# Loading x and w1 in other pieces, transposing x in pairs and running the first h groups side by side, at the start of a fused SiLU MLP forward and backward

## The chip, the cores and the metric

One core of one Trainium2 chip. The metric is device time of the program in microseconds (us), median of several executions. The profile's span is 1.7 to 2.0 us shorter than that time in all runs but one (2.35 us), because it begins with the first recorded instruction. All times inside the program are counted from the start of the span.

## The reference

Forward and gradients of a two-layer MLP in bfloat16, S = 2048 rows, D = 640, F = 1536:

```python
h   = einsum("bsd,df->bsf", x, w1)
out = einsum("bsf,fd->bsd", silu(h), w2)
# returned: out and the gradients of x, w1, w2 for a given grad_out
```

## The kernel before

TensorE does everything in 128x128 by 128x512 matmuls, 1,440 of them (the last 16 split in two). Rows are worked on in four chunks of 512. Chunk 0 first needs x transposed: four tiles of 128 rows are loaded, transposed on TensorE and copied out of PSUM, the memory that TensorE writes to, into `xT`. Then twelve groups of five matmuls make h. Everything later is long prefetched. These are the parts that matter, with cuts marked.

```python
# NWARM = 26 matmuls on a constant come first, to get TensorE's clock raised
load_x_tile(nc.sync, 0)            # 160 KB each; SyncE's and ScalarE's queue in turn
load_x_tile(nc.scalar, 1)
load_x_tile(nc.sync, 2)
load_x_tile(nc.scalar, 3)
for lo, hi in ((0, 2), (2, DT)):   # w1 rows in tiles of 128 (DT = 5), first 256 columns (FH)
    nc.sync.dma_start(out=w1_nat[:, lo:hi, 0:FH], in_=w1_v[:, lo:hi, 0:FH])
load_w1(FH, FC)                    # columns 256 to 512, all rows
# ... the rest of w1; w2 in two halves; transposed loads

def pe_x_tile(xT, st):             # one tile: 3 + 2 transposes, one copy for each part
    for lo, hi, copy in ((0, DS, nc.vector.tensor_copy), (DS, DT, nc.scalar.copy)):
        tp = ps_h.tile([P, hi - lo, P], dt_in, name="tp", tag="hp")
        for dt_ in range(lo, hi):
            nc.tensor.transpose(tp[:, dt_ - lo, :], x_nat[:, st, dt_ * P:(dt_ + 1) * P], ident[:])
        copy(out=xT[:, lo:hi, st * P:(st + 1) * P], in_=tp[:])

for st in range(STC):
    pe_x_tile(xT_next, st)
for i in range(NFILL):             # 4 fillers that keep TensorE busy
    nc.tensor.matmul(wp[:, 0:P], lhsT=ident[:], rhs=x_nat[:, STC - 1, 0:P], start=True, stop=True)
# ...
for ft in range(FT):               # chunk 0: twelve groups, one after the other
    h_group(ft, xT, aT, ghT)       # 5 matmuls over dt_, then silu, tanh, two VectorE steps
```

## Time and profile before

| | before |
|---|---|
| time, median of 3 runs | 322.19 us (321.62 to 322.34) |
| span of the profiled run | 320.5 us |
| first h matmul | 6.48 us |
| from there to the start of the last VectorE copy | 311.09 us, matmuls without a gap |
| busy share of TensorE | 98% |

The timeline of TensorE before (columns: start, duration, engine, line, operation, out<-in, shapes, count, and in brackets the idle time ahead of it and what ended it; a merged line's duration ends with its last, modelled matmul):

```profile
0.78 2.93 PE L96 MATMUL wp<-const-bfloat16-1.0 128*128 128x128 bf16 x26 [0.78 <-PEq L362]
3.62 0.74 PE L148 MATMUL tp<-ident,x_nat 128*128 128x128 bf16 x10
5.32 0.73 PE L148 MATMUL tp<-ident,x_nat 128*128 128x128 bf16 x10 [0.96 <-DMA x_nat<-in_x_dram]
5.88 0.39 PE L154 MATMUL wp<-x_nat,ident 128*128 128x128 bf16 x4
6.48 13.11 PE L161 MATMUL hp<-xT,w_nat 128*128 128x512 bf16 x58 [0.21 <-ACT xT L149]
19.43 13.11 PE L196 MATMUL hp<-aT,w_nat 128*128 128x512 bf16 x59
```

Phases follow each other at 12.95 us, which is 60 matmuls at 0.216 us. (The trace lacks a few matmul records: 58 and 59 of 60.) So whatever starts h earlier ends the program earlier, one for one. The chain of waits of the first 20 us before, from the x tile's transfer to h (start, duration, what; the lines ahead of and after these are left out, here and below):

```profile
1.19 4.09 DMA x_nat<-in_x_dram
5.27 0.05 issue
5.32 0.47 PE tp L148 x5
5.78 0.02 issue
5.81 0.66 ACT xT L149 x2
6.47 0.01 issue
6.48 0.38 PE hp L161
```

Tile 2 lands at 5.27 us, and from there it takes 1.2 us until h starts. (Tile 3 lands at 5.50 us, before its transposes begin at about 5.6 us, so it holds nothing up.) The issues of x tiles 2 and 3 before, on the two queues (size and us from the start of the issue, at about 1.2 us, to landing):

```profile
x_nat<-in_x_dram ACTq DMA_DIRECT2D x1, 160.0 KB, 4.3
x_nat<-in_x_dram SPq DMA_DIRECT2D x1, 160.0 KB, 4.1
```

### The profile page before, as it was taken

How to read it: one execution, taken by the hardware profiler on the slowest of the kernel's cores; microseconds unless marked ns; L12 is line 12 of the kernel's file. 1: busy time of each engine (PE TensorE's matmuls, PEld its weight loads, DVE VectorE, ACT ScalarE, POOL GpSimd, SP SyncE). 2: the span in 40 equal slices, each digit the busy share in tenths (PEclk: the TensorE clock that was granted, in tenths of full speed). 3: DMA queues.
4: the chain of work that ended last, by engine and by line, in shares of the span. 5: the costliest groups of instructions: out<-in, count | busy, mean ns of one | idle time of the engine just before them, and what ended most of it. 6: DMA issues, size and time to landing. Idle time of an engine off the chain costs nothing.

```text
span 320.5 us, 3556 instructions
## 1 busy us (share of the span) xinstructions
PE 314.0 (98%) x1477; PEld 145.9 (46%) x1506; DVE 101.8 (32%) x179; ACT 78.6 (25%) x142; POOL 0.7 (0%) x6
## 2 busy tenths in 40 slices
PE   7999999999999999999999999999999999999996
PEld 5444444444444444444444444444444444444443
DVE  1871551477510087810147741000000100001001
ACT  3960001555201255411054520110100001001100
POOL 0000000000000000000000000000000000000000
PEclk9999999999999999999999999999999999999999
DMA  8999999999699884392445079819999999995011
GB/s 246 316 192 209 254 265 253 320 271 277 215 229 336 203 237 122 118 319 66 127 159 141 2 254 268 217 25 293 262 240 263 249 203 343 251 281 181 33 49 35
DMA packets 149264, 66.69 MB, mean 208 GB/s; under 512 B 112640, under 2 KB 149248, under 8 KB 149248
## 3 DMA queue, kind: packets, MB, share of 16 engines
q1 hardware_dynamic: 148960, 66.13, 80.8%
q10 hardware_dynamic: 288, 0.33, 0.3%
q8 instruction: 12, 0.20, 0.2%
q14 instruction: 4, 0.03, 0.0%
HBM read 9.18 MB, written 28.97 MB: 119 GB/s over the span
## 4 chain that ended last, share of the span: by engine, by line
PE 97%; DMA 1%; issue 1%; ACT 0%; SPq 0%; DVE 0%; DVEq 0%
PE hp L196 32%; PE hp L180 16%; PE hp L286 16%; PE hp L161 16%; PE hp L334 15%; DMA x_nat<-in_x_dram 1%; PE hp L316 1%; ACT xT L149 0%; PE tp L148 0%; SPq L123 0%; DVE g_2366 L327 0%; DVEq L327 0%
## 5 line engine op out<-in xcount | busy, mean ns | idle before, releaser
L161 PE MATMUL hp<-xT,w_nat 128*128 128x512 bf16 x232 | 56.4, 379 | 0.6 <-ACT xT L149 0.2
L180 PE MATMUL hp<-goT,w2T 128*128 128x512 bf16 x238 | 56.8, 379 | 0.1
L196 PE MATMUL hp<-aT,w_nat 128*128 128x512 bf16 x235 | 52.2, 379 | 0.3
L196 PE MATMUL hp<-ghT,w1T 128*128 128x512 bf16 x235 | 52.2, 379 | 0.3
L286 PE MATMUL hp<-a_blk,go_nat 128*128 128x512 bf16 x236 | 51.8, 379 | 0.2
L334 PE MATMUL hp<-gh_blk,x_nat 128*128 128x512 bf16 x219 | 48.2, 379 | 0.3
L204 ACT ACTIVATE oT<-hp 128x512 bf16<-128x512 f32 x24 | 14.3, 597 | 110.0 <-PE hp L196 110.0
L168 ACT ACTIVATE aT<-hp 128x512 bf16<-128x512 f32 x48 | 28.7, 597 | 31.7 <-PE hp L161 31.7
L196 PEld LDWEIGHTS <-w_nat 128*128 128x128 bf16 x240 | 23.5, 98 | 28.3
L180 PEld LDWEIGHTS <-w2T 128*128 128x128 bf16 x240 | 23.5, 98 | 28.3
L286 PEld LDWEIGHTS <-go_nat 128*128 128x128 bf16 x240 | 23.5, 98 | 28.3
L161 PEld LDWEIGHTS <-w_nat 128*128 128x128 bf16 x240 | 23.4, 98 | 28.4 <-issue 0.4
L196 PEld LDWEIGHTS <-w1T 128*128 128x128 bf16 x240 | 23.4, 98 | 28.4
L206 DVE CAST oT<-hp 128x512 bf16<-128x512 f32 x16 | 11.1, 692 | 78.0 <-PE hp L196 78.0
L187 DVE SCALAR_TENSOR_TENSOR ghT<-ghT,hp 128x512 bf16<-128x512 bf16 x48 | 32.5, 682 | 7.3 <-PE hp L180 7.3
L334 PEld LDWEIGHTS <-x_nat 128*128 128x128 bf16 x224 | 21.9, 98 | 26.4
L173 DVE SCALAR_TENSOR_TENSOR ghT<-aT,v 128x512 bf16<-128x512 bf16 x48 | 33.0, 688 | 0.6
L172 DVE TENSOR_SCALAR v<-t 128x512 bf16<-128x512 f32 x48 | 20.5, 427 | 29.2 <-ACT t L170 29.2
L170 ACT ACTIVATE t<-hp 128x512 f32<-128x512 f32 x48 | 28.4, 591 | 0.0
L296 DVE CAST g2T<-hp 128x512 bf16<-128x512 f32 x7 | 4.8, 692 | 46.1 <-PE hp L286 46.1
L294 ACT ACTIVATE g2T<-hp 128x512 bf16<-128x512 f32 x8 | 4.8, 598 | 47.0 <-PE hp L286 40.7
L343 ACT ACTIVATE g_2140<-hp 128x512 bf16<-128x512 f32 x1 | 0.6, 597 | 13.6 <-DMA out_dram<-g_2077 13.6
(33 smaller groups left out, 29.3 us busy)
## 6 DMA issues: line engine op xcount, KB each, us to landing
aT_scr<-aT SPq DMA_DIRECT2D x4, 1536.0 KB, 6.7
ghT_scr<-ghT SPq DMA_DIRECT2D x4, 1536.0 KB, 8.0
out_dram<-o_sb SPq DMA_DIRECT2D x8, 640.0 KB, 3.4
oT_scr<-oT SPq DMA_DIRECT2D x4, 640.0 KB, 3.9
go_nat<-in_grad_out_dram SPq DMA_DIRECT2D x4, 640.0 KB, 8.1
gxT_scr<-oT SPq DMA_DIRECT2D x4, 640.0 KB, 4.7
w_nat<-in_w_dram SPq DMA_DIRECT2D x2, 960.0 KB, 10.9
x_nat<-in_x_dram SPq DMA_DIRECT2D x3, 640.0 KB, 7.8
```

The lines of the kernel that those rows point to most:

```text
L161: nc.tensor.matmul(hp[:], lhsT=w1_nat[:, dt_, ft * P:(ft + 1) * P], rhs=xT[:, dt_, :], start=(dt_ == 0), stop=(dt_ == DT - 1),)
L168: nc.scalar.activation(aT[:, ft, :], hp[:], ACT.Silu)
L170: nc.scalar.activation(t[:], hp[:], ACT.Tanh, scale=0.5)
L172: nc.vector.tensor_scalar(out=v[:], in0=t[:], scalar1=-0.5, scalar2=0.5, op0=ALU.mult, op1=ALU.add)
L173: nc.vector.scalar_tensor_tensor(out=ghT[:, ft, :], in0=aT[:, ft, :], scalar=1.0, in1=v[:], op0=ALU.subtract, op1=ALU.mult)
L180: nc.tensor.matmul(gp[:], lhsT=w2T[:, dt_, ft * P:(ft + 1) * P], rhs=goT[:, dt_, :], start=(dt_ == 0), stop=(dt_ == DT - 1),)
L187: nc.vector.scalar_tensor_tensor(out=ghT[:, ft, :], in0=ghT[:, ft, :], scalar=1.0, in1=gp[:], op0=ALU.add, op1=ALU.mult)
L196: nc.tensor.matmul(op_[:], lhsT=w_all[:, ft, dt_ * P:(dt_ + 1) * P], rhs=rhs_all[:, ft, :], start=(ft == 0), stop=(ft == FT - 1),)
L204: nc.scalar.activation(oT[:, dt_, :], op_[:], ACT.Copy)
L206: nc.vector.tensor_copy(out=oT[:, dt_, :], in_=op_[:])
L286: nc.tensor.matmul(gp[:], lhsT=go_nat[:, st, dt_ * P:(dt_ + 1) * P], rhs=a_blk[:, st, :], start=(st == 0), stop=(st == ST - 1),)
L334: nc.tensor.matmul(gp[:], lhsT=x_nat[:, st, dt_ * P:(dt_ + 1) * P], rhs=gh_blk[:, st, :], start=(st == 0), stop=(st == ST - 1),)
```

## The change

It means to use fewer and longer transfers, to need less of w1 before h starts, and to shorten the way from the last x tile to h. Tiles 2 and 3 come in one transfer. The first 512 columns of w1 come in row pieces: rows of tiles 0 and 1 (256 KB) on ScalarE's queue, rows of tiles 2 to 4 (384 KB) on SyncE's. Tiles are transposed in pairs, with one copy for each block of 128 columns, so that h may begin with the first block. The first four h groups do their first two matmuls side by side. Core of the diff:

```diff
-        load_x_tile(nc.sync, 0)
-        load_x_tile(nc.scalar, 1)
-        load_x_tile(nc.sync, 2)
-        load_x_tile(nc.scalar, 3)
-        for lo, hi in ((0, 2), (2, DT)):
-            nc.sync.dma_start(out=w1_nat[:, lo:hi, 0:FH], in_=w1_v[:, lo:hi, 0:FH])
-        load_w1(FH, FC)
+        load_x_tiles(nc.sync, 0, 1)
+        load_x_tiles(nc.scalar, 1, 2)
+        load_x_tiles(nc.sync, 2, STC)
+        load_w1_rows(nc.scalar, 0, KM)       # KM = 2
+        load_w1_rows(nc.sync, KM, DT)
 ...
-        (w2 in two halves)
+        nc.sync.dma_start(out=w2_nat[:], in_=w2_v[:])
 ...
-        (pe_x_tile for each of four tiles, then four fillers)
+        def pe_x_pair(xT, st):
+            for dt_ in range(DT):
+                tp = ps_h.tile([P, 2, P], dt_in, name="tp", tag="hp")
+                for q in range(2):
+                    nc.tensor.transpose(tp[:, q, :], x_nat[:, st + q, dt_ * P:(dt_ + 1) * P], ident[:])
+                copy = nc.scalar.copy if dt_ % 2 else nc.vector.tensor_copy
+                copy(out=xT[:, dt_, st * P:(st + 2) * P], in_=tp[:])
+        pe_x_pair(xT_next, 0)
+        (four fillers on the constant)
+        pe_x_pair(xT_next, 2)
 ...
+        def h_first(xT, aT, ghT):            # replaces the loop over h_group in chunk 0
+            hps = []
+            for ft in range(FB):             # FB = 4
+                hps.append(ps_h.tile([P, SC], FP32, name="hp"))
+            for dt_ in range(KM):
+                for ft in range(FB):
+                    h_mm(hps[ft], ft, xT, dt_, dt_ + 1)
+            for i in range(FT + LAG_G):      # LAG_G = 4: tanh and the rest lag behind silu
+                ...                          # rest of groups 0 to 3, then groups 4 to 11 whole
```

The scheduler puts the four fillers ahead of all transposes in TensorE's order.

More of the change, by code (lines that the diff above doesn't have):

```diff
@@ L41 @@
     STC = SC // P
-    DH = D // 2
     FC = 512
     NFC = F // FC
+    FB = FC // P
     LAG = 2
+    LAG_G = 4
+    KM = 2
     NWARM = 26
@@ L114, in load_goT @@
             return goT
-        FH = FC // 2
         xT_next = xpool.tile([P, DT, SC], dt_in, name="xT")
@@ L120, in load_w1, with load_x_tiles, load_w1_rows @@
             nc.sync.dma_start(out=w1_nat[:, :, lo:hi], in_=w1_v[:, :, lo:hi])
-        def load_x_tile(eng, st):
-            eng.dma_start(out=x_nat[:, st, :], in_=x_v[:, st, :])
-        load_x_tile(nc.sync, 0)
-        load_x_tile(nc.scalar, 1)
-        load_x_tile(nc.sync, 2)
-        load_x_tile(nc.scalar, 3)
-        for lo, hi in ((0, 2), (2, DT)):
-            nc.sync.dma_start(out=w1_nat[:, lo:hi, 0:FH], in_=w1_v[:, lo:hi, 0:FH])
-        load_w1(FH, FC)
+        def load_x_tiles(eng, lo, hi):
+            eng.dma_start(out=x_nat[:, lo:hi, :], in_=x_v[:, lo:hi, :])
+        def load_w1_rows(eng, lo, hi):
+            eng.dma_start(out=w1_nat[:, lo:hi, 0:FC], in_=w1_v[:, lo:hi, 0:FC])
+        load_x_tiles(nc.sync, 0, 1)
[3 more added lines that the diff above has]
+        load_w1_rows(nc.sync, KM, DT)
         for fc in range(1, NFC):
@@ L134 @@
         nc.scalar.activation(warm_a[:], warm[:, 0:1], ACT.Silu)
-        for hf in range(2):
-            nc.sync.dma_start(out=w2_nat[:, :, hf * DH:(hf + 1) * DH], in_=w2_v[:, :, hf * DH:(hf + 1) * DH])
+        nc.sync.dma_start(out=w2_nat[:], in_=w2_v[:])
         goT_next = load_goT(0)
@@ L140, with h_mm @@
         nc.sync.dma_start_transpose(out=w1T[:], in_=w1[:, :])
-        DS = 3
-        def pe_x_tile(xT, st):
-            for lo, hi, copy in ((0, DS, nc.vector.tensor_copy), (DS, DT, nc.scalar.copy)):
-                tp = ps_h.tile([P, hi - lo, P], dt_in, name="tp", tag="hp")
-                for dt_ in range(lo, hi):
-                    nc.tensor.transpose(tp[:, dt_ - lo, :], x_nat[:, st, dt_ * P:(dt_ + 1) * P], ident[:])
-                copy(out=xT[:, lo:hi, st * P:(st + 1) * P], in_=tp[:])
-        for st in range(STC):
-            pe_x_tile(xT_next, st)
-        for i in range(NFILL):
-            nc.tensor.matmul(
-                wp[:, 0:P], lhsT=ident[:], rhs=x_nat[:, STC - 1, 0:P], start=True, stop=True
-            )
-        def h_group(ft, xT, aT, ghT):
-            hp = ps_h.tile([P, SC], FP32, name="hp")
-            for dt_ in range(DT):
+        def pe_x_pair(xT, st):
[6 more added lines that the diff above has]
+        pe_x_pair(xT_next, 0)
+        for i in range(NFILL):
+            nc.tensor.matmul(wp[:, 0:P], lhsT=warm, rhs=warm, start=True, stop=True)
+        pe_x_pair(xT_next, 2)
+        def h_mm(hp, ft, xT, lo, hi):
+            for dt_ in range(lo, hi):
                 nc.tensor.matmul(
@@ L167, in h_group, with silu_a, silu_grad @@
                 )
+        def silu_a(ft, hp, aT):
             nc.scalar.activation(aT[:, ft, :], hp[:], ACT.Silu)
+        def silu_grad(ft, hp, aT, ghT):
             t = tpool.tile([P, SC], FP32, name="t")
@@ L175, in h_group @@
             )
+        def h_group(ft, xT, aT, ghT):
+            hp = ps_h.tile([P, SC], FP32, name="hp")
+            h_mm(hp, ft, xT, 0, DT)
+            silu_a(ft, hp, aT)
+            silu_grad(ft, hp, aT, ghT)
+        def h_first(xT, aT, ghT):
[6 more added lines that the diff above has]
+            for i in range(FT + LAG_G):
+                if i < FT:
+                    if i < FB:
+                        h_mm(hps[i], i, xT, KM, DT)
+                    else:
+                        hps.append(ps_h.tile([P, SC], FP32, name="hp"))
+                        h_mm(hps[i], i, xT, 0, DT)
+                    silu_a(i, hps[i], aT)
+                if i >= LAG_G:
+                    silu_grad(i - LAG_G, hps[i - LAG_G], aT, ghT)
         def g_group(ft, goT, ghT):
@@ L226 @@
             if c == 0:
-                for ft in range(FT):
-                    h_group(ft, xT, aT, ghT)
+                h_first(xT, aT, ghT)
                 nc.sync.dma_start(
@@ L277 @@
         g2T_v = g2T_scr[:].rearrange("(dt p) f -> p dt f", p=P)
-        FB = FC // P
         k = 0
```

## The prediction

> **What bounds the kernel now.** TensorE. In its timeline the first h matmul starts at 6.48 us, and from there each 128x512 matmul follows the last at 0.216 us until 317.5 us; 1,440 x 0.216 = 311 us is the whole stretch. In the view of waits TensorE waits for nothing after 6.48 us. So the change, which touches only the start, can move the first h matmul or open a gap in a stream that has none. At most about 1 us of 322 can be won.
>
> **What sets 6.48 us.** The chain of waits: issue of an x tile (0.74), its DMA until 5.27 us, transposes 0.47, two ScalarE copies 0.66, h. By the DMA view the x tiles land at about 3.5, 3.7, 5.3 and 5.5 us, the pieces of w1 at 5.8, 6.4 and 7.4, each ahead of its use. DMA share is 0.99 or more from 2.5 us on. In the trace's packet records nearly all x packets are done by 4.1 us; one straggling DMA engine, alternating between the SyncE and ScalarE queues at about 0.052 us a packet, ends tiles 2 and 3 at 4.84 and 4.95; landings follow 0.45 us later.
>
> **What the change does.**
> 1. Same bytes, other order. 256 KB of w1 now stand on ScalarE's queue behind tile 1, beside tiles 2 and 3 (320 KB) on SyncE's. The Trainium skill, "DMA: Bandwidth & Descriptors", section "Queues, rings and completion order", says each DMA engine round-robins between queues by packet; the trace agrees (the straggler's alternation). So 16 w1 packets of 1,024 B get between the last x packets of each engine: 16 x 0.044 = 0.7 us (estimate from 0.052 us for 1,280 B). Tiles 2 and 3 land at about 6.1 us, the first w1 rows with them: a loss of 0.6 to 0.8 us.
> 2. The route from there to h gets shorter. Before: 5.3 to 6.48 = 1.17 us (transposes, fillers, copies of 0.36 and 0.37 us). After: ten transposes at 0.056 us; the first four h matmuls need only dt 0's copy on VectorE, about 0.25 us, done as the tenth transpose ends. About 0.65 us: a gain of 0.5. The fillers now come before the transposes and cost nothing.
> 3. Rows 2 to 4 of w1 are needed only after 8 matmuls (about 8.5 us); they land at about 7.4.
> 4. ScalarE gets its first group 2.4 us after h starts instead of 1.2: 23 activations at about 0.54 us put the last silu 14 to 14.8 us after the start; the second product asks for it at 15.3. No stall, little slack.
> 5. w2 in one DMA should land by about 17.5 us (before: 15.2 and 17.7); needed at 19.4.
>
> Later chunks keep their order. So h starts at about 6.75 us (6.2 to 7.1): +0.3, discounted a little because the queues' sharing may favour x.
>
> **Predicted: 322.4 us, 321.5 to 323.2.** Faster by over 2%: 0.004; within 2%: 0.986; slower: 0.01.
>
> **What would show it.** First h matmul at 6.6 to 6.9 us; tiles 2 and 3 landing near 6.1; TensorE idle about 1.5 us between the two batches of transposes; 0.65 us from the last landing to h; no gap after the 8th h matmul nor at the first w2 matmul; the rest shifted as one block.
>
> **What would make it wrong.** x served ahead of w1 (h at 6.2, 321.9 us); w1 rows 2 to 4 late; the last silu late; the idle stretch dropping TensorE's clock, granted in full only from 3.7 us.

## The result, and the profile after

| | before | after |
|---|---|---|
| time, 4 runs each | 322.21 us (321.62 to 322.34) | 321.54 us (321.52 to 321.68) |
| ratio of the fast runs | | 0.9984, interval 0.9966 to 1.0001 |
| first h matmul, profiled run | 6.48 us | 5.87 us |
| h to the start of the last VectorE copy | 311.09 us | 311.09 us |

A ratio is the mean time of one kernel's fast runs over that of the other's of the same rounds, so not quite the ratio of the medians. The timeline of TensorE after, with the columns of before:

```profile
0.77 2.93 PE L98 MATMUL wp<-const-bfloat16-1.0 128*128 128x128 bf16 x26 [0.77 <-PEq L385]
3.50 0.52 PE L153 MATMUL wp<-const-bfloat16-1.0 128*128 128x128 bf16 x4
3.85 0.72 PE L147 MATMUL tp<-ident,x_nat 128*128 128x128 bf16 x10
5.20 0.73 PE L147 MATMUL tp<-ident,x_nat 128*128 128x128 bf16 x10 [0.62 <-DMA x_nat<-in_x_dram]
5.87 13.11 PE L158 MATMUL hp<-xT,w_nat 128*128 128x512 bf16 x60
18.82 13.11 PE L221 MATMUL hp<-aT,w_nat 128*128 128x512 bf16 x60
```

The chain of waits of the first 24 us after:

```profile
1.19 3.96 DMA x_nat<-in_x_dram
5.16 0.05 issue
5.20 0.73 PE tp L147 x10
5.93 13.05 PE hp L158 x60
```

The DMA issues after (the same columns; the first two start at 1.17 to 1.2 us, the last at 1.66 us):

```profile
x_nat<-in_x_dram SPq DMA_DIRECT2D x1, 320.0 KB, 4.0
w_nat<-in_w_dram ACTq DMA_DIRECT2D x1, 256.0 KB, 4.3
...
w_nat<-in_w_dram SPq DMA_DIRECT2D x1, 384.0 KB, 5.2
```

From the landing that h waits for to h takes 0.71 us instead of 1.2 us, as foretold. But the tiles landed at 5.16 us, not at 6.1. One profile on each side cannot say whether the second fact belongs to the change, so the first experiments repeat both kernels.

### The profile page after: what moved, and what is told of

It reads as the page before. It is cut to its first block, busy times and chain, and to the rows that moved or that the text cites. A ratio compares the mean times of both kernels' runs of the same rounds, so it can differ in the third digit from the quotient of the medians.

```text
span 319.7 us, 3584 instructions
## 1 busy us (share of the span) xinstructions
PE 315.5 (99%) x1506; PEld 146.0 (46%) x1506; DVE 101.5 (32%) x181; ACT 77.5 (24%) x142; POOL 0.7 (0%) x6
## 4 chain that ended last, share of the span: by engine, by line
PE 98%; DMA 1%; SPq 0%; DVE 0%; issue 0%; DVEq 0%
PE hp L221 32%; PE hp L158 16%; PE hp L309 16%; PE hp L205 16%; PE hp L357 15%; DMA x_nat<-in_x_dram 1%; PE hp L339 1%; PE tp L147 0%; SPq L124 0%; DVE g L350 0%; DVEq L350 0%
## 5 line engine op out<-in xcount | busy, mean ns | idle before, releaser
L167 ACT ACTIVATE aT<-hp 128x512 bf16<-128x512 f32 x48 | 30.0, 627 | 32.6 <-PE hp L158 32.6
L171 ACT ACTIVATE t<-hp 128x512 f32<-128x512 f32 x48 | 29.9, 628 | 0.0
L368 DVE CAST g<-hp 128x512 bf16<-128x512 f32 x7 | 4.8, 692 | 47.0 <-PE hp L357 25.8
```

What stands on the lines that cost most here:

```text
L167: nc.scalar.activation(aT[:, ft, :], hp[:], ACT.Silu)
L171: nc.scalar.activation(t[:], hp[:], ACT.Tanh, scale=0.5)
```

## The experiments

All outputs are right. Each run had 5 rounds. "h at" is the start of the first h matmul in the profiled execution.

| run | what | this, median (range) us | ratio (interval) | h at |
|---|---|---|---|---|
| e1 | before again | 322.12 (321.44 to 322.56) | 0.9997 (0.9986 to 1.0009) | 5.68 |
| e2 | after again | 321.80 (321.32 to 324.12) | 1.0000 (0.9975 to 1.0024) | 7.22 |
| e3 | before, paired transposes | 321.47 (321.31 to 321.79) | 0.9981 (0.9969 to 0.9993) | 5.63 |
| e4 | after, w1 rows on SyncE's queue | 322.19 (321.93 to 322.38) | 1.0002 (0.9990 to 1.0013) | 6.79 |
| e5 | before, the new loads | 322.69 (322.00 to 323.82, and one at 684.22) | 1.0022 (1.0007 to 1.0037) | disturbed |
| e6 | after, h one group after the other | 322.25 (321.89 to 322.47) | 1.0005 (0.9993 to 1.0017) | 5.91, then a wait |
| e7 | e3, another closing semaphore | 321.60 (320.93 to 322.20) | 0.9984 (0.9972 to 0.9996) | 6.11, then a wait |
| e8 | after, tile 3 ahead of the w1 rows | 326.47 (323.74 to 327.05) | 1.0118 (1.0086 to 1.0149) | 8.09 |
| e9 | e7, two groups side by side | 321.77 (321.44 to 322.24) | 0.9998 (0.9987 to 1.0010) | 5.99 |
| e10 | e9 without fillers | 321.53 (321.06 to 322.62) | 0.9999 (0.9984 to 1.0014) | 5.60 |
| e11 | after, a third time | 321.77 (321.38 to 324.39) | 1.0011 (0.9986 to 1.0035) | 6.18 |
| e12 | e3 again | 321.76 (321.60 to 321.82) | 0.9991 (0.9978 to 1.0005) | 5.99 |

### e1 and e2: both kernels again

No edit.

> The kernel before, unchanged, for the spread of its landings. Theory A (the straggling DMA engine of the first profile was hit by chance by one packet of about 0.40 us at 3.9 us): tiles 2 and 3 land earlier in this profile, near 5.1 us, and the first h matmul starts near 6.1 us; times spread by about 0.5 us. Theory B (the late landing belongs to this order of loads): last x tiles land again at 5.3 to 5.5 us, h starts at 6.4 to 6.6 us. Ratio 1.000 in both.

> The changed kernel, unchanged, for the spread of its landings and a tighter ratio. Theory A: tiles 2 and 3 land between 5.1 and 5.6 us, the first h matmul between 5.8 and 6.3 us, ratio 0.998 to 0.9995. Theory B: landing at 5.15 us again and h at 5.9 us, ratio about 0.998.

The chain of waits of e1, the kernel before unchanged:

```profile
0.77 2.93 PE wp L96 x26
3.71 0.68 PE tp L148 x5
4.38 0.02 issue
4.41 1.26 ACT xT L149 x4
5.67 0.01 issue
5.68 0.38 PE hp L161
```

No DMA stands on it. Tiles 2 and 3 landed at 4.5 and 4.7 us, 0.8 us earlier than in the first profile of the same program:

```profile
x_nat<-in_x_dram ACTq DMA_DIRECT2D x1, 160.0 KB, 3.5
x_nat<-in_x_dram SPq DMA_DIRECT2D x1, 160.0 KB, 3.3
```

And the changed kernel, whose tiles landed at 5.16 us at first, had them at 6.5 us in e2, with h at 7.22 us. Its chain of waits:

```profile
1.20 5.31 DMA x_nat<-in_x_dram
6.51 0.05 issue
6.55 0.73 PE tp L147 x10
```

In the packet records of the trace a transfer's share of one DMA engine goes by in steady steps of about 0.05 us, broken by single packets that take 0.2 to 1.9 us (the longest at 6.20 us in e12). In the first profile of before, one packet of 0.40 us at 3.9 us is among them; in e2, one of 1.08 us at 4.43 us is among the w1 packets. A tile has landed when the slowest of 16 engines is done. In e2 the w1 rows on ScalarE's queue were finished by ten engines before 5.0 us and by the last at 6.65 us. So theory A holds: the landing of one execution is a draw, and a single profile of each kernel compares two draws. The half of theory A that a repeat of the changed kernel would land by 5.6 us missed, because the spread is wider than I gave it. Its ratio of 1.0000 missed both theories too.

TensorE's clock is a second draw. The trace shows it granted in full from 3.67 us (before), 3.75 (after), 5.25 (e2), 5.87 us (e11); until then a transpose takes 0.107 us instead of 0.056.

### e3 and e12: paired transposes alone

```diff
-        for st in range(STC):
-            pe_x_tile(xT_next, st)
-        (four fillers on x)
+        pe_x_pair(xT_next, 0)
+        (four fillers on the constant)
+        pe_x_pair(xT_next, 2)
```

> The kernel before with only the transposes changed: tiles transposed in pairs with one copy for each of five column blocks, the fillers ahead of them; loads and the h groups as before. If the gain is the shorter route from the last x landing to h: from landing to h 0.65 us instead of 1.0 to 1.2, h at 5.9 to 6.1 us, time 0.4 to 0.5 us under the kernel before (ratio about 0.9985). If the gain is the new order of loads: the route is shorter but the last tile (the ScalarE one, at 5.5 us) holds it, h at 6.2 us or later, ratio 0.9992 or above.

> The kernel before with paired transposes alone, a second time, because the spread between runs is as large as the effects. If paired transposes are what wins: a median 0.2 to 0.6 us under the kernel before of the same rounds, ratio 0.998 to 0.9995, no run over 322.6 us. If the first result was a lucky draw: ratio 0.9995 to 1.0005.

Both repeats are under the kernel before, by 0.19% and 0.09% (the second interval includes 1), and none of the ten runs is over 321.82 us. This part of the change alone brings what the change brings. The way is shorter in every profile: from the start of the last transpose to h it is 0.65 us in before and e1, and 0.06 to 0.18 us wherever transposes are paired and h waits for no w1 (after, e2, e3, e6, e9 to e12). What is left of it depends on the draw. In e3 the later tile landed at 4.96 us, h came at 5.63; in e1, where it landed at 4.66, h came at 5.68. When tiles are early the four fillers take part of the gain back: ahead of the transposes, they move the first of these from 3.66 (e1) to 3.93 us (e3). The chain of waits of e3:

```profile
3.71 0.43 PE wp L152 x4
4.13 1.55 PE tp L146 x20
5.68 1.40 PE hp L158 x6
```

The expected value was met; the reason is not always the one expected. The chain of waits of e12:

```profile
0.77 2.93 PE wp L96 x26
3.70 0.43 PE wp L152 x4
4.13 2.02 PE tp L146 x20
6.16 13.02 PE hp L158 x60
```

Here all tiles had landed by 4.6 us and TensorE itself is the chain, as its clock came only at 5.91 us: 20 transposes take 2.02 us, and the four fillers, which now stand ahead of them, take 0.43 us.

### e4: the w1 rows on SyncE's queue

```diff
-        load_w1_rows(nc.scalar, 0, KM)
+        load_w1_rows(nc.sync, 0, KM)
```

> The changed kernel, but the 256 KB of w1 go to SyncE's queue behind tiles 2 and 3 instead of ScalarE's beside them. If the sharing of the queues delays the tiles (the prediction's step 1, half a microsecond or so): tiles 2 and 3 land at 4.6 to 4.8 us, and then w1 decides, landing at about 5.5 us as before, h at 5.6 to 5.9 us. If the sharing costs the tiles nothing: they land at 5.1 to 5.2 us as in the changed kernel, w1 0.3 us or more after them, h at 6.0 us or later.

The tiles landed at 4.9 us, between the two expectations. Then w1 decided, but at 6.74 us and not at 5.5. The waits of TensorE in e4 (waiter, what it waited for, total us, times, longest):

```profile
PE hp L158 <- DMA w_nat<-in_w_dram: 1.1, 1, 1.1
```

ScalarE's queue does bring the first w1 rows earlier; it costs the tiles something.

How much, the undisturbed landings tell (left out are before, e9 and e2 as disturbed, and e4, 4.9 us). Without w1 beside them, the later of tiles 2 and 3 landed at 4.7 (e1), 5.0 (e3), 4.5 (e7), 4.6 (e8), 4.6 (e10) and 4.6 us (e12). With w1 beside them it was 5.16 (after), 5.2 (e5), 5.2 (e6) and 5.1 us (e11). That is 0.5 us for sharing. As this picks among landings, here is a check that picks none: the trace has one semaphore update for each of the 16 engines of a transfer, and their median is not moved by a straggler. For the later of tiles 2 and 3 it stands at 4.28 to 4.49 us in all nine profiles without w1 beside the tiles (before, e9 and e4 among them) and at 4.75 to 4.88 us in all five with it (e2 among them). In e4 tiles 2 and 3 are one transfer, as in the changed kernel, with a median at 4.28 us: so the size of the transfer is not the reason.

### e5 and e6: the new loads with the old compute, and the changed kernel without side by side groups

e5 has the load part of the diff only. e6 is the changed kernel with:

```diff
-                h_first(xT, aT, ghT)
+                for ft in range(FT):
+                    h_group(ft, xT, aT, ghT)
```

> The changed kernel's loads with the transposes and the h groups of the kernel before. Theory: the loads alone win nothing, the route from the last x landing to h stays at 1.0 to 1.2 us and the second half of w1 (rows 2 to 4) is asked for only 0.43 us after h starts, so h starts at 6.2 to 6.6 us or stalls; the end is 0.17 us shorter because the program has three transfers fewer and the last one uses another semaphore. Time 0.2 us under to 0.4 us over the kernel before (ratio 0.9994 to 1.0013). Rival, the loads are what won: ratio 0.9985 or less.

> The changed kernel with its first h groups one after the other. If side by side groups hide the landing of w1 rows 2 to 4: here the third h matmul waits, as w1 rows 2 to 4 land at about 6.8 us and h starts at 5.9, so a stall of about 0.4 us and a time 0.3 to 0.5 us over that of the changed kernel (ratio to the kernel before about 0.9995 to 1.0005). If they hide nothing: no stall, the same time as the changed kernel (ratio 0.998 to 0.999).

The new loads alone make the kernel slower, by 0.22%, more than the theory's range. The profiled execution of e5 was disturbed: h matmuls came 0.443 us apart instead of 0.216 from start to end, so that 60 took 28 us instead of 13 (684.22 us in all). Its trace holds no record of the clock, and the cause is open. It stands outside the ratio, and nothing but the landings above is taken from it.

e6 has no side by side groups, and its chain of waits goes through the second row piece of w1:

```profile
1.66 4.94 DMA w_nat<-in_w_dram
6.59 0.05 issue
6.64 12.69 PE hp L158 x58
```

h starts at 5.91 us, does two matmuls, and stands until 6.64 us, a stall of 0.3 us. The expectation was 0.4. So side by side groups hide this stall. The whole times do not show it (1.0005 against 0.9984, 1.0000 and 1.0011 of the changed kernel). They do not beat the old loads, where the piece that is needed second is 192 KB instead of 384.

### e7: the end of the program

The program closes with five checks on SyncE, each on one or two semaphores. A semaphore is a counter that a transfer raises when it lands. Transfers take eight of them in turn, so three transfers fewer move the last store from the third semaphore to the zeroth.

```text
closing checks in order: (3,2) (4,1) (5,0) (6,VectorE) (7,ScalarE)
                          start of each check, us                        drain
before, semaphore 3:      319.376 319.445 319.512 319.576 319.638        319.703
after, semaphore 0:       317.664 317.733 317.799* 318.789 318.851       318.916
e9, semaphore 7:          317.778 317.848 317.914 318.284 318.849        318.914
* lasts 953 ns: it waits there for the last store
```

Before, all checks come after the last landing; after, only two do. Merging away four loads of later chunks puts the store on semaphore 7:

```diff
-                for j in range(0, ST, STC):
-                    nc.sync.dma_start(out=go_nat[:, j:j + STC, :], in_=go_v[:, j:j + STC, :])
+                for j in range(0, ST, 2 * STC):
+                    nc.sync.dma_start(out=go_nat[:, j:j + 2 * STC, :], in_=go_v[:, j:j + 2 * STC, :])
 ...
-                (x_nat for chunks 1 to 3 in three transfers)
+                nc.sync.dma_start(out=x_nat[:, STC:ST, :], in_=x_v[:, STC:ST, :])
```

> The kernel before with the paired transposes alone, and four load transfers of later chunks merged away, so that the last store's semaphore moves from the first of SyncE's five closing checks to the last. If the checks after the last landing cost 0.066 us each: the stretch from the last landing to the end of the program shortens by 0.26 us and the time is 321.2 us, ratio to the kernel before about 0.997. If the 0.17 us seen between the kernels' ends has another cause: 321.45 us as paired transposes alone, ratio 0.998.

From the first h matmul to the end of the span it is 313.98 us before, in e1 and in e3 (313.97), 313.80 after and in e2, 313.67 in e9 and 313.69 in e10, which carry this edit too. So the change gained 0.18 us at its far end without meaning to, and e7's edit gains 0.30 us. The whole time of e7 doesn't show it against e3, perhaps because its start drew worse: in its profile h waited for w1's first piece until 6.11 us and, after two matmuls, for its second until 6.82.

### e8: no w1 packet ahead of an x packet

```diff
-        load_x_tiles(nc.sync, 2, STC)
+        load_x_tiles(nc.sync, 2, 3)
+        load_x_tiles(nc.scalar, 3, 4)
```

> The changed kernel, with tile 3 on ScalarE's queue ahead of its w1 rows, so that no w1 packet is queued ahead of an x packet. If sharing the queues delays the tiles by 0.3 to 0.5 us as worked out from the packet records: the last tiles land at about 4.7 to 5.0 us with 0.5 us less spread, h at 5.5 to 5.8 us unless w1 rows 0 and 1 are late, time 0.2 to 0.4 us under the changed kernel. If stalls of single packets alone decide: no difference from the changed kernel beyond its spread (321.3 to 322.8 us).

The tiles did land early, at 4.4 and 4.6 us. But the 256 KB of w1, issued at 1.67 us instead of 1.17, landed at 8.04 us. The chain of waits of e8:

```profile
1.67 6.37 DMA w_nat<-in_w_dram
8.04 0.05 issue
8.09 12.04 PE hp L159 x55
```

Four of the six runs are slower still, over 326 us, at a granted clock of 0.988 to 0.995; none of them is profiled. In the profiled run eleven DMA engines had finished these rows by 5.89 us and the other five between 6.92 and 7.73 us. In the changed kernel all sixteen finish between 4.50 and 5.09 us. The rows are issued half a microsecond later and land 2.5 us later. That the issue time is the cause is not shown: they also stand behind one more tile, and SyncE's queue holds 384 KB and more of w1 issued at the same time. The five engines had hardly begun: of the 80 packets that are their share of 256, at most a handful start before 5.8 us. At least three engines were as late with SyncE's 384 KB (updates at 6.98, 7.45 and 8.13 us, the other thirteen by 6.10), so that it is not, or not only, a matter between the two queues. Why they are so late was not settled.

### e9, e10 and e11: a candidate, and the changed kernel a third time

e9 joins e7 with side by side groups, but only two, so that the old loads suffice; e10 sets NFILL to 0.

```diff
+    NSIDE = 2            # in h_first, in place of FB
-                for ft in range(FT):
-                    h_group(ft, xT, aT, ghT)
+                h_first(xT, aT, ghT)
```

> A candidate: loads of the start as in the kernel before, paired transposes, only the first two h groups side by side (they need just the first 256 columns of w1), and the last store's semaphore at SyncE's last check. If the parts add: h starts at 5.6 to 5.9 us as with paired transposes alone, w1 rows 2 to 4 are asked for 0.86 us later and cause no stall in most runs, 0.26 us less at the end: 321.1 to 321.3 us, ratio 0.9965 to 0.9975. If stalled packets swamp it: 321.5 us or more.

> The same candidate without the four filler matmuls, which in the runs with early tiles stand between the tiles and their transposes. If they are on the chain: h 0.2 to 0.4 us earlier in runs with early tiles, median 320.9 to 321.1 us. If the tiles' landing decides, or the clock is granted later without them: the same as the candidate with fillers, or slower by 0.2 us.

> The changed kernel a third time, for its ratio and its spread. If the first two results are draws from one wide distribution: a median of 321.5 to 321.9 us with at least one of six runs over 322.5 us, ratio 0.998 to 1.000. If the slow runs of the second were an accident of that chip or hour: all runs within 321.4 to 321.8 us.

e9 and e10 missed: 0.9998 and 0.9999 against an expected 0.9970. The parts are there (no stall in h, 0.30 us less at the end, and e10's best run of 321.06 us), but the whole time doesn't show them. That the draws at the start swamp them is likely, not shown: there is one profile of each. e9's profile has one ScalarE tile landing at 5.33 us. Its chain of waits:

```profile
1.17 4.17 DMA x_nat<-in_x_dram
5.33 0.05 issue
5.38 0.68 PE tp L149 x9
```

e11 confirms e2: one of six runs is at 324.39 us (the ratio, 1.0011, lies above what was expected). Pooled over all (which ran on different chips, so only a rough picture):

| | runs | median | mean | highest |
|---|---|---|---|---|
| before | 52 | 322.01 | 321.99 | 322.65 |
| after | 16 | 321.65 | 322.02 | 324.39 |
| paired transposes alone | 10 | 321.67 | 321.63 | 321.82 |

The change shifts the usual run by about 0.35 us to the better and gives it all back in the mean by a few runs of 322.8 to 324.4 us. Paired transposes alone keep the gain without those runs; of the versions run, that is the one I would keep. The slow runs go with the new loads: the 79 runs with the old ones (these 52 and 10, and e7, e9, e10) have none above 322.65 us, e5 has three besides the disturbed one and the changed kernel three, though e4 and e6 have none in five each. The gain itself is small against the spread: only the intervals of e3 and e7 exclude 1, and e9 and e10, which also pair, show none.

## Why the prediction was right or wrong

The forecast of 322.4 us (321.5 to 323.2) held: 321.54 us at first, 321.65 us over 16 runs. Its direction, 0.2 us slower, was not borne out: the ratios are 0.9984, 1.0000 and 1.0011. The hit itself says little: a range of 1.7 us would have held had the change done nothing.

- **What bounds the kernel** was right. In before, after, e1, e2 and e3 alike, 311.09 us pass from the first h matmul to the start of the last VectorE copy. Only the two ends can differ.
- **Step 1, x delayed by sharing**, is the step that failed: "Tiles 2 and 3 land at about 6.1 us". They landed at 5.16 (5.1 to 5.2 in e5, e6 and e11, 6.5 in e2). The mechanism was right and its size nearly so: 0.5 us measured, 0.6 to 0.8 forecast. (By 4.4 us, with 11 of the 384 packets of SyncE's x tiles still to end, 148 of the 256 w1 packets had begun: 9 for each engine, not the 16 of the forecast; at the 0.046 us of such a packet that is an estimated 0.4 us.) What was wrong was the term it was added to. The 5.3 and 5.5 us of the profile of before were taken as the kernel's landing; they were one disturbed draw, where undisturbed landings are 4.5 to 5.0 us. The prediction named the "straggling DMA engine" and still treated it as fixed.
- **The skill's round-robin**: the Trainium skill, "DMA: Bandwidth & Descriptors", section "Queues, rings and completion order", says that each DMA engine alternates between queues by packet. The trace agrees: on the engine that is last before, packets of the two queues start in turn at 4.67, 4.72, 4.78 and 4.83 us, and the half microsecond of sharing fits. In e8 ScalarE's 256 KB took 6.37 us to land beside SyncE's; as the late engines began late, that decides nothing about the sharing.
- **Step 2, the shorter route**, was right: 0.65 us forecast, 0.71 us measured, against 1.2 before. e3 and e12, which change only this and the place of the fillers, show that it is the gain. "The fillers now come before the transposes and cost nothing" was wrong in executions with early tiles: there they stand on the chain for 0.43 us (e12) and start the transposes 0.27 us later. Leaving them out (e10) gave no gain clear of the noise.
- **Step 3** was right: rows 2 to 4 landed at 6.8 us, ahead of their use at about 7.6. e6 shows what the side by side groups hide, 0.3 us.
- **Steps 4 and 5** were right: TensorE goes from h to the next product without a gap (5.87 + 12.95 = 18.82 us). The last silu ended at 19.82 us, 14.0 us after h began. w2 landed at 16.7 us.
- **Not foreseen**: 0.18 us at the end, from a semaphore's place in the closing checks, and the late grant of the clock in some executions. The idle stretch did not drop the clock; the grant itself is what varies.

## What to carry to other kernels

When a kernel is one unbroken stream of matmuls, only its first and last microseconds can move, and there a transfer lands when the slowest of 16 engines is done: look at several executions of the kernel before you add a cost to a landing read from one. Put the work that follows the last landing first (which copy does the first matmul really need?), as that way, unlike the landings, was shorter in every profile. A second queue need not bring a transfer forward: in e8 the same 256 KB, behind one more tile and issued half a microsecond later, landed 2.5 us later.

## What the Trainium skill lacked or had wrong

- "DMA: Bandwidth & Descriptors", section "Queues, rings and completion order": nothing there lets one foretell that some engines begin a transfer late. In e8 five of 16 engines finished 256 KB on ScalarE's queue 1.0 to 1.8 us after the last of the other eleven, and the transfer landed 6.37 us after its issue.
- The same page has no figure for how far single packets of one transfer differ: 0.2 to 1.9 us against some 0.05 us here, the likely reason that moved the landing of one transfer of an unchanged kernel from 4.7 to 5.5 us (before), and from 5.2 to 6.5 us (after).
- The same page, section "Specifications", gives a first-byte latency of about 0.6 us for transfers issued by SyncE and ScalarE; it doesn't say from where it counts. Here the first packet starts at about 1.76 us in every profile, for an issue that runs from 0.74 to 1.14 us: 1.0 us from its start, 0.6 us, in agreement, from its end.
- "TensorE: Matmul & The Clock Gate", Part 1, has the clock raised about 4 us into sustained matmuls, give or take 0.5 us. Matmuls here begin at 0.78 us and the full clock came between 3.67 and 6.12 us (e8), 2.9 to 5.3 us later, in the twelve profiles with a record of it: a spread of 2.5 us, not 1. (The same Part's free-running activity window of about 3.4 us would leave room for that.)
- No page that I found has the cost of the closing checks: 0.066 us each on SyncE, 0.18 us between two kernels that differ by three transfers.
